# An attention and channel-mix kernel on one core: the first weights asked for in ScalarE's queue, key buffers without gaps, first zero fills on VectorE

## The chip, the cores and the metric

The kernel runs on one core of a Trainium2 chip. The metric is device time in microseconds (us) of one execution, lower is better; the time of the kernel before is the median of three runs. Engines: PE is TensorE (PEld its weight loads), DVE is VectorE, ACT is ScalarE, POOL is GpSimd, SP is SyncE, which here only issues transfers. ACT can issue transfers too, in a queue of its own.

## The reference

Four batches, eight heads, 768 positions, head size 64. Attention with a local window of 96 positions and 8 global positions and a linear position bias, and on its output, with the heads side by side (512 wide), a channel mix:

```
scores = scale * q @ k.T + bias;  scores = where(keep, scores, -1e9)
a = exp(scores - max);  a = a / (sum(a) + 1e-09);  x = a @ v
xk = mu_k * x + (1 - mu_k) * x_prev;  xr = mu_r * x + (1 - mu_r) * x_prev
k = maximum(xk @ w_k, 0);  v = k * k @ w_v;  r = sigmoid(xr @ w_r)
out = r * v
```

w_k is 512 x 1024, w_v 1024 x 512, w_r 512 x 512. They come as float64, two 32-bit words for each number.

## The kernel before

The 3072 positions are 24 tiles of 128 rows. For each tile the queries and keys of all heads are loaded in transposed form (64 partitions, 8 heads x 128), scored on PE two heads at a time (L313, L314), biased and reduced on DVE (L322, with a table `pat`, or `pat0` for the first tile of a batch), exponentiated on ACT (L323), scaled on ACT and POOL (L334, L336), transposed on PE and copied by ACT (L348, L350), and multiplied by v (L367). The first eight tiles ("native") score straight from the loaded tiles: queries go to two buffers `qz`, keys to a ring of three `kz`. These buffers have 128 partitions, of which the loads fill 64; the other 64 are zeroed once (L223, L226, on POOL). Two of the three key buffers are cut out of wider tiles (128 of 232 columns per head), so their rows consist of eight pieces of 512 bytes.

Two tiles make a chunk of the channel mix (`ffn`): mixing with the position before on ACT or POOL and DVE (L391, L393, L394), a split into a high part on ACT (`xk_hi`, L395) and a low part on DVE (`xk_lo`, L396), and then three matmuls for each product (L403 to L405): 96 for `kp` (w_k) and, with 512 columns each, 24 for `z` (w_r) and 48 for `vps` (w_v). Steps of `ffn` are woven between the attention steps of later tiles; the first `ffn` begins with tile 3 (`LAG`).

The weights come in ten loads of 1 MB: four of w_k (`w_0` to `w_3`), two of w_r, four of w_v, each turned from float64 words into two float32 halves by `weight_begin` and `weight_end`: ACT takes the absolute value (L172, L175), POOL (for w_k, L173) or DVE (L176) clamps it, DVE shifts and merges (L177, L178, L179), ACT rounds the high part (L181) and DVE subtracts it (L187). W_LOADS says how many loads are asked for at each step of the program (four steps a tile), W_BEGUN how many are begun.

All loads go through SP's queue, in program order per buffer. A transfer is issued only when a transfer that used the same one of eight counters (every eighth of either queue, about) has landed. The order on each engine is set when the kernel is built, by a scheduler that works with times of its own; on the chip every engine goes through its list strictly in order.

Of the kernel before, what the change touches and what calls it, by code (L numbers as in the profile page):

```python
# [9 lines left out]
F32 = mybir.dt.float32  # L10
F32R = mybir.dt.float32r
BF16 = mybir.dt.bfloat16
I32 = mybir.dt.int32
U32 = mybir.dt.uint32
AF = mybir.ActivationFunctionType
# [4 lines left out]
B, H, S, D = 4, 8, 768, 64  # L20
# [8 lines left out]
W = GMAX + BACK + 128  # L29
# [1 line left out]
LATE = 128 - OWN  # L31
NEG = -1.0e9

W_LOADS = (2, 2, 2, 2, 3, 3, 4, 4, 4, 5, 5, 6, 6, 7, 7, 8, 8, 9, 9, 10)
W_BEGUN = (1, 1, 2, 2, 3, 3, 4, 4, 4, 5, 5, 6, 6, 6, 7, 7, 8, 8, 9, 9, 10)
GAP = {"kk_hi": 16, "xk_lo": 96, "xr_lo": 16}
FAR = 1.0e12
# [4 lines left out]
def tile_biased_attention_channel_mix(ctx: ExitStack, tc: tile.TileContext, qT, kT, v, n_sizes, mu_kr, w_k, w_v, w_r, q_rows, k_rows, v_rows, slopes, out):  # L42
    nc = tc.nc
    vec, act, pool, pe = nc.vector, nc.scalar, nc.gpsimd, nc.tensor

    const = ctx.enter_context(tc.tile_pool(name="const", bufs=1))
# [27 lines left out]
    kw_pool = fast.enter_context(tc.tile_pool(name="kw", bufs=2))  # L74
# [6 lines left out]
    f_pool = fast.enter_context(tc.tile_pool(name="fp", bufs=1))  # L81
# [7 lines left out]
    zeros = const.tile([128, 512], BF16, name="zeros")  # L89
# [5 lines left out]

    pat = const.tile([128, H, W], BF16, name="pat")
    pat0 = const.tile([128, H, 128], BF16, name="pat0")
    f_pool.tile([128, 96], F32, name="ahead", tag="ahead")  # L100
    btmp = f_pool.tile([128, 2048 + GAP["kk_hi"]], F32, name="btmp", tag="kk_hi")
    cut = iter((0, 352, 704, 928, 1056, 1184, 1184 + W))
    edge = [next(cut)]
# [1 line left out]
    def piece():  # L105
        edge.append(next(cut))
        return btmp[:, edge[-2] : edge[-1]]

    ints, flts, local, glo, dist0, dist = (piece() for _ in range(6))
    ints = ints.bitcast(I32)  # L110
    j = flts[:, 224:352]
# [14 lines left out]
    vec.scalar_tensor_tensor(dist0, glo, nlf, local[:, 96:224], op0=ALU.max, op1=ALU.min)  # L126
    for h in range(H):
        c = -8.0 * 2.0 ** -(h + 1)
        if h < 6:
            vec.tensor_scalar(pat0[:, h, :], dist0, c, None, op0=ALU.mult)  # L130
        else:
            pool.tensor_scalar(pat0[:, h, :], dist0, c, 1.0, op0=ALU.mult, op1=ALU.mult)
# [6 lines left out]
    for h in range(H):  # L139
        c = -8.0 * 2.0 ** -(h + 1)  # L140
# [2 lines left out]
        else:  # L143
            pool.tensor_scalar(pat[:, h, :], dist, c, 1.0, op0=ALU.mult, op1=ALU.mult)
    pool.tensor_scalar(mus1, mus, -1.0, 1.0, op0=ALU.mult, op1=ALU.add)

    w_steps = [(name, src, j) for name, src, pairs in (("k", w_k, 4), ("r", w_r, 2), ("v", w_v, 4)) for j in range(pairs)]
    w_raw, w_live = {}, {}

    def weight_load(i):  # L150


        name, src, j = w_steps[i]
        raw = w_raw[i] = const.tile([128, 1024, 2], I32, tag=f"w{i}", name=f"w64_{i}")
        if name == "k":
            ins = nc.sync.dma_start(raw.rearrange("p n w -> p (n w)"), src[j * 128 : (j + 1) * 128, :])
        else:
            ins = nc.sync.dma_start(raw.rearrange("p (k n) w -> p k (n w)", k=2), src[j * 256 : (j + 1) * 256, :].rearrange("(k p) m -> p k m", p=128))
        tc.keep_in_program_order(ins)

    def weight_begin(i):

# [26 lines left out]
            kn = both if name == "k" else both[:, :, k * 512 : (k + 1) * 512]  # L189
            wts[name, j if name == "k" else 2 * j + k] = kn[:, 0, :], kn[:, 1, :]  # L190

    w_count = [0, 0, 0]

    def weights_load(n):
        while w_count[2] < min(n, len(w_steps)):
            weight_load(w_count[2])
            w_count[2] += 1

    def weights_go(begun, ended):
        weights_load(begun)  # L200
        while w_count[0] < min(begun, len(w_steps)):
            weight_begin(w_count[0])
            w_count[0] += 1
        while w_count[1] < min(ended, w_count[0]):
            weight_end(w_count[1])
            w_count[1] += 1
# [11 lines left out]
    q_zero, k_ring = [], []  # L218
    for i in range(3):
        if i < 2:  # L220
            q_zero.append(q_pool.tile([128, H, 128], F32, name=f"qz_{i}", tag="qh"))
            kz = kw_pool.tile([128, H, W], F32, name=f"kz_{i}", tag="kw")[:, :, 0:128]
            pool.memset(q_zero[i][64:128], 0.0)  # L223
        else:
            kz = q_pool.tile([128, H, 128], F32, name=f"kz_{i}", tag="ql")
        pool.memset(kz[64:128], 0.0)  # L226
        k_ring.append(kz)
    k_first = const.tile([64, H, GMAX], F32, name="k_first")

# [244 lines left out]
    for step in range(NTILES + 1):  # L474
        if step + 1 < NTILES:
            load_tile(step + 1)
        if step == 0:
            load_v(0)
        if step < NATIVE:
            first_keys(step)  # L480
        for hp in range(4):
            if hp == 0 and step > 1:
                for i in range(4):
                    weighted(step - 2, i)
            if hp == 0 and 0 < step < NTILES:
                load_v(step)
            if step:
                transposes(step - 1, hp)
            if step < NTILES:
                scores(step, hp)  # L490
            if hp == 0:
                if step >= LAG and (step - LAG) % 2 == 0:
                    queue.append(ffn((step - LAG) // 2))
                    if len(queue) == 1 and step == LAG:
                        budget[0] = -17.5
            run_ffn(2.5)
            run_ffn(2.5)
            if hp == 1 and step + 1 < NTILES:
                split_tile(step + 1)
            slot = 4 * step + hp  # L500
            weights_load(W_LOADS[min(slot, len(W_LOADS) - 1)])
            n = W_BEGUN[min(slot, len(W_BEGUN) - 1)]
            weights_go(n, n - 1 if slot < len(W_BEGUN) else n)
# [172 lines left out]
```

## Time and profile before

| | us |
|---|---|
| median of 3 runs (511.41 to 511.92) | 511.73 |
| the profiled execution, its own time | 511.73 |
| its span, first to last instruction | 510.0 |
| PE busy in the span | 488.9 |
| DVE busy | 346.6 |
| ACT busy | 338.0 |
| POOL busy | 215.3 |

A timeline row has start, duration, engine, line, operation, what is written and read, and in brackets the idle time of the engine before it and what ended that. A duration includes the end of the pipeline, so that instructions in a row overlap a little; what one costs its engine is the distance between two starts. The granted clock of PE is 1.00 at 2.4 GHz and 0.50 at 1.2 GHz.

### The profile page before, as it was taken

Reading aid. Unit: us, or ns where it says so; the run is one execution under the profiler, and the core shown is the slowest. Engines: PE = TensorE matmul, PEld = TensorE weight load, DVE = VectorE, ACT = ScalarE, POOL = GpSimd, SP = SyncE. Lnnn points to the kernel's source line nnn. Section 1 sums busy time; section 2 is a strip of 40 time slices with the busy share of each in tenths; the row PEclk is TensorE's granted clock in tenths of the full one; section 3 lists DMA queues with packets and bytes.
Section 4 is the critical chain, followed back from the end, with each engine's and each line's share of the span. In section 5 each row is a group of like instructions: output and inputs, shape, how many; then the busy total and the mean of one; then the engine's idle time right before and its main releaser. Section 6 shows DMA issues by size and latency. Waiting matters only on the chain.

```text
span 510.0 us, 10113 instructions
## 1 busy us (share of the span) xinstructions
PE 488.9 (96%) x3562; PEld 431.8 (85%) x3562; DVE 346.6 (68%) x826; ACT 338.0 (66%) x826; POOL 215.3 (42%) x359
## 2 busy tenths in 40 slices
PE   7858998999999999999999999999999999999995
PEld 4647987898898898898898898898898898898984
DVE  6999989755468777757768767757768765535321
ACT  4998999757548759567668577567668578554220
POOL 7341216243348546527538536527538535203000
PEclk9888999999999999999999999999999999999999
DMA  8998511513842433433433333433323221100101
GB/s 225 321 247 248 204 42 39 121 43 78 173 91 78 104 101 81 103 100 78 107 84 79 104 102 78 104 100 79 106 82 80 64 60 39 41 1 2 41 2 46
DMA packets 24041, 49.46 MB, mean 97 GB/s; under 512 B 5008, under 2 KB 9104, under 8 KB 23472
## 3 DMA queue, kind: packets, MB, share of 16 engines
q1 hardware_dynamic: 23840, 48.74, 35.5%
q8 instruction: 30, 0.49, 0.4%
q14 instruction: 27, 0.22, 0.1%
q10 hardware_dynamic: 144, 0.00, 0.0%
HBM read 42.44 MB, written 6.29 MB: 96 GB/s over the span
## 4 chain that ended last, share of the span: by engine, by line
PE 85%; DMA 7%; DVE 3%; ACT 2%; issue 1%; POOL 1%; SPq 1%; POOLq 0%; DVEq 0%
PE kp L403 8%; PE vps L405 8%; PE vps L404 8%; PE vps L403 8%; PE kp L405 8%; PE kp L404 8%; PE av L367 7%; PE t L348 7%; DMA qz<-in_qT_dram 5%; PE z L403 4%; PE z L404 4%; PE z L405 4%; PE s L317 3%; PE s L316 3%; PE s L314 2%; PE s L313 1%
## 5 line engine op out<-in xcount | busy, mean ns | idle before, releaser
L336 POOL TENSOR_SCALAR e<-e,r 128x232 f32<-128x232 f32 (+1 forms) x168 | 83.1, 513 | 162.2 <-DVE r L330 130.2
L403 PE MATMUL kp<-xk_hi,wk 128*128 128x256 f32 x384 | 108.4, 283 | 2.0 <-ACT xk_hi L395 2.0
L404 PE MATMUL kp<-xk_lo,wk 128*128 128x256 f32 x384 | 107.3, 280 | 0.0
L405 PE MATMUL kp<-xk_hi,wk 128*128 128x256 f32 x384 | 107.2, 279 | 0.0
L323 ACT ACTIVATE e<-e,nmax 128x232 f32<-128x232 f32 (+1 forms) x192 | 89.6, 470 | 22.7 <-DVE nmax L322 22.1
L322 DVE CUSTOM_DVE_ANT_0 e<-s,pat 128x232 f32<-128x232 f32 (+1 forms) x192 | 64.6, 374 | 22.8 <-PE s L317 14.3
L405 PE MATMUL vps<-wv,kk_lo 128*128 128x512 f32 x192 | 75.3, 392 | 0.0
L403 PE MATMUL vps<-wv,kk_hi 128*128 128x512 f32 x192 | 75.2, 394 | 0.0
L404 PE MATMUL vps<-wv,kk_hi 128*128 128x512 f32 x192 | 75.2, 392 | 0.0
L403 PEld LDWEIGHTS kp<-xk_hi,wk 128*128 128x128 f32 x384 | 72.0, 188 | 3.0 <-ACT xk_hi L395 2.2
L404 PEld LDWEIGHTS kp<-xk_lo,wk 128*128 128x128 f32 x384 | 72.1, 188 | 0.4
L405 PEld LDWEIGHTS kp<-xk_hi,wk 128*128 128x128 f32 x384 | 72.1, 188 | 0.0
L431 DVE TENSOR_TENSOR kk<-kp,kk 128x512 f32<-128x512 f32 x48 | 33.1, 689 | 46.5 <-ACT kk L430 46.3
L350 ACT COPY et<-t 128x256 f32<-128x256 f32 (+1 forms) x176 | 56.3, 373 | 8.2 <-PE t L348 7.6
L348 PE MATMUL t<-ident,e 128*128 128x128 f32 x352 | 54.5, 276 | 0.9 <-ACT e L334 0.7
L348 PEld LDWEIGHTS t<-ident,e 128*128 128x128 f32 x352 | 40.2, 136 | 9.7 <-ACT e L334 0.9
L367 PE MATMUL av<-et,va 128*64 128x128 f32 x384 | 42.7, 287 | 4.4 <-ACT et L350 4.2
L433 DVE TENSOR_TENSOR kk_lo<-kk,kk_hi 128x512 fp32r<-128x512 f32 x48 | 34.6, 722 | 17.5 <-ACT kk_hi L432 17.1
L430 ACT ACTIVATE kk<-kp 128x512 f32<-128x512 f32 x48 | 28.4, 591 | 24.5 <-PE kp L405 24.3
L432 ACT CAST kk_hi<-kk 128x512 fp32r<-128x512 f32 x48 | 29.8, 623 | 20.9 <-DVE kk L431 20.1
L405 PEld LDWEIGHTS vps<-wv,kk_lo 128*128 128x128 f32 x192 | 36.0, 188 | 7.7
L404 PEld LDWEIGHTS vps<-wv,kk_hi 128*128 128x128 f32 x192 | 36.2, 188 | 6.9
(101 smaller groups left out, 1067.0 us busy)
## 6 DMA issues: line engine op xcount, KB each, us to landing
qraw<-in_qT_dram SPq DMA_DIRECT2D x32, 256.0 KB
kraw<-in_kT_dram SPq DMA_DIRECT2D x32, 256.0 KB
out_dram<-sig SPq DMA_DIRECT2D x24, 256.0 KB
va<-in_v_dram SPq DMA_DIRECT2D x20, 240.0 KB
vb<-in_v_dram SPq DMA_DIRECT2D x20, 208.0 KB
w<-in_w_k_dram SPq DMA_DIRECT2D x4, 1024.0 KB
w<-in_w_v_dram SPq DMA_DIRECT2D x4, 1024.0 KB
qz<-in_qT_dram SPq DMA_DIRECT2D x8, 256.0 KB
```

The lines of the kernel that those rows point to most:

```text
L322: vec.tensor_tensor_reduce(out=e[:, :w], in0=o, in1=p[:, h, :], op0=ALU.add, op1=ALU.min, scale=-0.125, scalar=3.0e38, accum_out=s["nmax"] ...
L323: act.activation(e[:, :w], e[:, :w], AF.Exp, bias=s["nmax"][:, h : h + 1], scale=-1.0, accum_out=s["sum"][:, h : h + 1])
L336: pool.tensor_scalar(e[:, :w], e[:, :w], r[:, u : u + 1], 1.0, op0=ALU.mult, op1=ALU.mult)
L348: pe.transpose(pt[0:p, c : c + 128], e[:, k * 128 : k * 128 + p], ident)
L350: act.copy(et[0:p, k * 256 : k * 256 + 256], pt[0:p, k * 256 : k * 256 + 256])
L367: pe.matmul(o, vt[:, h * 64 : (h + 1) * 64], et[0:p, c + q : c + 128], start=k == 0, stop=k == nb - 1)
L403: pe.matmul(o, sh, mh, start=first, stop=False)
L404: pe.matmul(o, sh, ml, start=False, stop=False)
L405: pe.matmul(o, sl, mh, start=False, stop=last)
L431: vec.tensor_mul(kk, pv, kk)
L432: act.copy(kkh[:, 2 * fp : 2 * fp + 2, :], kk)
L433: vec.tensor_sub(kkl[:, 2 * fp : 2 * fp + 2, :], kk, kkh[:, 2 * fp : 2 * fp + 2, :])
```

## The change

The four loads of w_k are issued by ACT instead of SP, all of them ahead of the program's loop and behind a tiny activation (`warm`) that brings the activation table in. W_LOADS asks for w_r and w_v some steps earlier. The two key buffers that were cut from wider tiles are now one run of 1024 columns in the same tiles. Zero fills of the first query and first key buffer go from POOL to DVE. Of the eight heads of `pat0`, the four odd ones go to ACT (three from DVE, one from POOL). Two tiles that only fill space (`ahead`) are added or widened. Moved text is left out here:

```diff
-W_LOADS = (2, 2, 2, 2, 3, 3, 4, 4, 4, 5, 5, 6, 6, 7, 7, 8, 8, 9, 9, 10)
+W_LOADS = (4, 4, 4, 4, 4, 4, 5, 5, 6, 6, 7, 7, 8, 8, 9, 9, 10)
...
+    warm = const.tile([128, 1], F32, name="warm")
+    act.activation(warm, zeros[:, 0:1], AF.Exp)
...
+        raw = w_raw[i] = w_home[i]
         if name == "k":
-            ins = nc.sync.dma_start(raw.rearrange("p n w -> p (n w)"), src[j * 128 : (j + 1) * 128, :])
+            ins = nc.scalar.dma_start(raw.rearrange("p n w -> p (n w)"), src[j * 128 : (j + 1) * 128, :])
...
+    const.tile([128, 96], F32, name="ahead")
+    w_home = [const.tile([128, 1024, 2], I32, tag=f"w{i}", name=f"w64_{i}") for i in range(len(w_steps))]
+    weights_load(4)
...
-    f_pool.tile([128, 96], F32, name="ahead", tag="ahead")
+    f_pool.tile([128, 128], F32, name="ahead", tag="ahead")
...
-        if h < 6:
+        if h % 2:
+            act.mul(pat0[:, h, :], dist0, c)
+        elif h < 6:
             vec.tensor_scalar(pat0[:, h, :], dist0, c, None, op0=ALU.mult)
...
-            kz = kw_pool.tile([128, H, W], F32, name=f"kz_{i}", tag="kw")[:, :, 0:128]
-            pool.memset(q_zero[i][64:128], 0.0)
+            kz = kw_pool.tile([128, H, W], F32, name=f"kz_{i}", tag="kw").rearrange("p h w -> p (h w)")[:, 0 : H * 128]
+            kz = kz.rearrange("p (h w) -> p h w", h=H)
+            (pool if i else vec).memset(q_zero[i][64:128], 0.0)
...
-        pool.memset(kz[64:128], 0.0)
+        (pool if i else vec).memset(kz[64:128], 0.0)
```

The scheduler moves more than the diff says. On SP, from the first weights on, stood this before (`w_0` to `w_3` are w_k, `w_4` and `w_5` w_r; the first `qz_172` row is the queries of tile 2, `qz_176` those of tile 3):

```order
L156 DMA w_0_201<-in_w_k_dram 128x2048
L156 DMA w_1_203<-in_w_k_dram 128x2048
L258 DMA kz_180<-in_kT_dram 64x1024
L270 DMA va_268<-in_v_dram 8x512
L271 DMA va_268<-in_v_dram 120x512
L272 DMA vb_269<-in_v_dram 104x512
L250 DMA qz_172<-in_qT_dram 64x1024
L156 DMA w_2_289<-in_w_k_dram 128x2048
L156 DMA w_3_341<-in_w_k_dram 128x2048
L272 DMA vb_391<-in_v_dram 104x512
L158 DMA w_4_442<-in_w_r_dram 128x2x1024
L158 DMA w_5_498<-in_w_r_dram 128x2x1024
```

and now (`qz_189` is the queries of tile 2, `qz_193` those of tile 3, `kz_190` and `kz_194` the keys of tiles 3 and 4; `w_6` is the first load of w_v):

```order
L282 DMA vb_282<-in_v_dram 104x512
L112 DMA w_4_141<-in_w_r_dram 128x2x1024
L282 DMA vb_401<-in_v_dram 104x512
L112 DMA w_5_142<-in_w_r_dram 128x2x1024
L112 DMA w_6_143<-in_w_v_dram 128x2x1024
L260 DMA qz_189<-in_qT_dram 64x1024
...
L280 DMA va_400<-in_v_dram 8x512
L281 DMA va_400<-in_v_dram 120x512
L268 DMA kz_190<-in_kT_dram 64x1024
L260 DMA qz_193<-in_qT_dram 64x1024
L268 DMA kz_194<-in_kT_dram 64x1024
L260 DMA qz_189<-in_qT_dram 64x1024
```

The queries of tile 2 stood behind two weight loads and now stand behind both of w_r and the first of w_v as well, with the four of w_k in the other queue.

On ACT, ahead of the rounding of the first mixed activations (`xk_hi`), stood this before (`wa_629` is the load `w_6`):

```order
L350 COPY et_0_536<-t_0_535 128x256
L350 COPY et_0_536<-t_0_535 104x256
L350 COPY et_1_581<-t_1_580 128x256
L350 COPY et_1_581<-t_1_580 104x256
L175 ACTIVATE wa_629<-w_6_608 128x1024
L323 ACTIVATE e_2_593,sum_440<-e_2_593,nmax_441 128x232
L395 CAST xk_hi<-mix_k 128x1024
```

and now (`wa_771` is the load `w_7`, `wv_643` the high part of `w_6`):

```order
L197 CAST wv_643<-wa_637 128x1024
L360 COPY et_0_544<-t_0_543 128x256
L360 COPY et_0_544<-t_0_543 104x256
L360 COPY et_1_590<-t_1_589 128x256
L360 COPY et_1_590<-t_1_589 104x256
L344 ACTIVATE e_4_475<-e_4_475,r_3_501 128x232
L344 ACTIVATE e_5_478<-e_5_478,r_3_501 128x232
L191 ACTIVATE wa_771<-w_7_144 128x1024
L405 CAST xk_hi<-mix_k 128x1024
```

`xk_hi` stood behind the absolute value of `w_6`, and now stands behind the rounding of `w_6` and the absolute value of `w_7`.

On DVE, ahead of the low part `xk_lo`, stood this before (`wa_444` is `w_4`, `wa_500` is `w_5`, `wa_629` is `w_6`):

```order
L179 SCALAR_TENSOR_TENSOR wa_444<-w_4_442,wa_444 128x1024
L322 ISA e_4_623,nmax_441<-s_2_618,pat 128x232
...
L176 TENSOR_SCALAR wa_500<-wa_500 128x1024
L322 ISA e_5_626,nmax_441<-s_2_618,pat 128x232
...
L176 TENSOR_SCALAR wa_629<-wa_629 128x1024
L322 ISA e_6_651,nmax_441<-s_3_646,pat 128x232
...
L322 ISA e_7_654,nmax_441<-s_3_646,pat 128x232
...
L177 TENSOR_SCALAR wa_500<-wa_500 128x1024
L396 TENSOR_TENSOR xk_lo<-mix_k,xk_hi 128x1024
```

and now (`wa_637` is `w_6`, `wr_514` the low part of `w_5`, `wa_771` is `w_7`):

```order
L194 SCALAR_TENSOR_TENSOR wa_637<-w_6_143,wa_637 128x1024
L203 TENSOR_TENSOR wr_514<-wa_508,wr_514 128x1024
...
L195 SCALAR_TENSOR_TENSOR wa_637<-w_6_143,wa_637 128x1024
L404 SCALAR_TENSOR_TENSOR mix_k<-x_397,mus,mix_k 128x256 x3
...
L332 ISA e_5_633,nmax_452<-s_2_625,pat 128x232
...
L203 TENSOR_TENSOR wv_643<-wa_637,wv_643 128x1024
L192 TENSOR_SCALAR wa_771<-wa_771 128x1024
L193 TENSOR_SCALAR wa_771<-wa_771 128x1024
L406 TENSOR_TENSOR xk_lo<-mix_k,xk_hi 128x1024
```

Before, `w_4` was not yet subtracted there and `w_5` and `w_6` had only their clamps (and `w_5` its shift); now `w_4`, `w_5` and `w_6` are finished and `w_7` has its clamp and shift, all ahead of `xk_lo`. At the start, ACT has the step of `w_0` (L188 in the new numbering, L172 before) ahead of its first exponential, where it had it behind all eight and two scalings.

## Rows read from the trace of the kernel before

**Rows 1.** The page's heads: the span; busy time of the engines; by 40 slices, the granted clock of PE.

```profile
span 510.0 us, 10113 instructions
...
PE 488.9 (96%) x3562; PEld 431.8 (85%) x3562; DVE 346.6 (68%) x826; ACT 338.0 (66%) x826; POOL 215.3 (42%) x359
...
PEclk9888999999999999999999999999999999999999
```

**Rows 2.** Busy time by stretches of the span: stretch, its length, busy time (instructions) of PE, PEld, DVE, ACT, POOL, granted clock, share of the DMA engines, GB/s.

```profile
10.00:20.00 10.00, 7.23 (x56) 5.94 (x55) 7.66 (x35) 9.90 (x37) 4.02 (x8) 1.00 1.04 321
30.00:40.00 10.00, 5.18 (x35) 4.47 (x36) 9.69 (x17) 9.83 (x27) 5.09 (x6) 0.72 1.06 187
40.00:50.00 10.00, 7.87 (x60) 6.45 (x59) 9.70 (x27) 7.56 (x20) 0.66 (x2) 0.94 0.86 261
60.00:80.00 20.00, 20.00 (x153) 17.68 (x152) 17.93 (x41) 18.93 (x41) 5.61 (x9) 1.00 0.28 82
80.00:100.00 20.00, 18.66 (x137) 15.59 (x136) 16.44 (x42) 16.95 (x46) 8.95 (x14) 1.00 0.37 83
100.00:130.00 30.00, 30.00 (x208) 26.33 (x208) 17.80 (x41) 20.42 (x45) 9.68 (x18) 1.00 0.21 60
160.00:460.00 300.00, 300.00 (x2254) 269.78 (x2253) 206.74 (x488) 203.68 (x500) 146.08 (x246) 1.00 0.31 83
```

**Rows 3.** PE's waits in the first 60 us: line and operand, what ended the wait, us in total, times, the longest.

```profile
PE s L313 <- DMA qz<-in_qT_dram: 4.7, 2, 2.4
...
PE kp L403 <- ACT xk_hi L395: 2.0, 1, 2.0
```

**Rows 4.** The timeline around the first matmuls of the channel mix (`kp`).

```profile
46.53 1.15 ACT L175 ACTIVATE wa<-w 128x1024 f32<-128x1024 f32 x1 [2.44 <-DVE nmax L322]
...
48.05 1.03 ACT L395 CAST xk_hi<-mix_k 128x1024 fp32r<-128x1024 f32 x1
...
49.14 0.63 PE L403 MATMUL kp<-xk_hi,wk 128*128 128x256 f32 x3 [2.01 <-ACT xk_hi L395]
...
49.56 1.22 DVE L396 TENSOR_TENSOR xk_lo<-mix_k,xk_hi 128x1024 fp32r<-128x1024 f32 x1
...
53.35 0.36 PE L404 MATMUL kp<-xk_lo,wk 128*128 128x256 f32 x1
```

**Rows 5.** DVE's timeline at the start: the zeros for the first dummy matmuls, the sizes, six heads of `pat0`, the first bias-and-minimum of tile 0.

```profile
0.87 0.27 DVE L90 MEMSET zeros<- 128x256 uint32 x1 [0.87 <-PEq L666]
...
4.14 0.56 DVE L57 CAST words<-sizes_w 128x4 f32<-128x4 int32 x1 [2.14 <-DMA sizes_w<-in_n_sizes_dram]
...
7.58 1.31 DVE L130 TENSOR_SCALAR pat<-btmp 128x128 bf16<-128x128 f32 x6
...
9.08 0.28 DVE L322 CUSTOM_DVE_ANT_0 e<-s,pat 128x128 f32<-128x128 f32 x1
```

**Rows 6.** ACT's timeline: the table, four heads of `pat`, and the first steps of `w_0` and of `w_3`.

```profile
1.16 1.28 ACT L142 ACT_TABLE_LOAD   x1 [1.16 <-PEq L666]
7.63 1.25 ACT L142 ACTIVATE pat<-btmp 128x232 bf16<-128x232 f32 x4 [5.18 <-DVE btmp L136]
...
13.29 1.13 ACT L172 ACTIVATE wa<-w 128x1024 f32<-128x1024 f32 x1
...
28.37 1.21 ACT L172 ACTIVATE wa<-w 128x1024 f32<-128x1024 f32 x1
```

**Rows 7.** The timeline where SP issues `w_0` and `w_1`, and where PE gets the queries of tile 2 and of tile 3.

```profile
4.40 0.91 SPq L156 DMA_DIRECT2D w<-in_w_k_dram  x2
...
20.16 0.44 PE L313 MATMUL s<-kz,qz 128*128 128x104 f32 x2 [2.37 <-DMA qz<-in_qT_dram]
...
37.73 0.72 PE L313 MATMUL s<-kz,qz 128*128 128x104 f32 x2 [2.37 <-DMA qz<-in_qT_dram]
```

**Rows 8.** Stretches of 1 us, columns as in rows 2: keys and queries of the first tiles under way, then w_k alone, then PE after its wait for tile 3.

```profile
6.00:7.00 1.00, 0.17 (x1) 0.20 (x2) 0.98 (x7) 0.00 (x0) 0.94 (x3) 1.00 0.96 157
...
10.00:11.00 1.00, 1.00 (x8) 1.00 (x7) 0.31 (x4) 1.00 (x6) 0.00 (x0) 1.00 1.08 451
...
38.00:39.00 1.00, 1.00 (x6) 1.00 (x6) 1.00 (x3) 1.00 (x3) 1.00 (x2) 0.50 0.96 158
...
41.00:42.00 1.00, 1.00 (x10) 1.00 (x9) 1.00 (x2) 1.00 (x3) 0.00 (x0) 0.86 1.01 213
```

**Rows 9.** DVE's timeline, instructions back to back: two heads of a later tile, shift, merges and subtraction of weights, and two that took longer than their like.

```profile
18.60 1.00 DVE L329 TENSOR_SCALAR r<-sum 128x4 f32<-128x4 f32 x1
...
26.16 0.39 DVE L322 CUSTOM_DVE_ANT_0 e<-s,pat 128x232 f32<-128x232 f32 x1
26.48 0.40 DVE L322 CUSTOM_DVE_ANT_0 e<-s,pat 128x232 f32<-128x232 f32 x1
...
29.88 2.05 DVE L178 SCALAR_TENSOR_TENSOR wa<-w,wa 128x1024 int32<-128x1024 int32 x1
...
32.49 0.68 DVE L177 TENSOR_SCALAR wa<-wa 128x1024 int32<-128x1024 int32 x1
33.09 0.15 DVE L329 TENSOR_SCALAR r<-sum 128x4 f32<-128x4 f32 x1
33.17 1.21 DVE L179 SCALAR_TENSOR_TENSOR wa<-w,wa 128x1024 int32<-128x1024 int32 x1
34.30 1.21 DVE L178 SCALAR_TENSOR_TENSOR wa<-w,wa 128x1024 int32<-128x1024 int32 x1
```

More of the change, by code (lines that the diff above doesn't have):

```diff
@@ L93, in tile_biased_attention_channel_mix, with weight_load, weights_load @@
         pe.matmul(idle, zeros[:, 0:128], zeros, start=True, stop=True)
+    warm = const.tile([128, 1], F32, name="warm")
+    act.activation(warm, zeros[:, 0:1], AF.Exp)
+    w_steps = [(name, src, j) for name, src, pairs in (("k", w_k, 4), ("r", w_r, 2), ("v", w_v, 4)) for j in range(pairs)]
+    w_raw, w_live = {}, {}
+    def weight_load(i):
+        name, src, j = w_steps[i]
+        raw = w_raw[i] = w_home[i]
+        if name == "k":
+            ins = nc.scalar.dma_start(raw.rearrange("p n w -> p (n w)"), src[j * 128 : (j + 1) * 128, :])
+        else:
+            ins = nc.sync.dma_start(raw.rearrange("p (k n) w -> p k (n w)", k=2), src[j * 256 : (j + 1) * 256, :].rearrange("(k p) m -> p k m", p=128))
+        tc.keep_in_program_order(ins)
+    w_count = [0, 0, 0]
+    def weights_load(n):
+        while w_count[2] < min(n, len(w_steps)):
+            weight_load(w_count[2])
+            w_count[2] += 1
+    const.tile([128, 96], F32, name="ahead")
+    w_home = [const.tile([128, 1024, 2], I32, tag=f"w{i}", name=f"w64_{i}") for i in range(len(w_steps))]
+    weights_load(4)
     pat = const.tile([128, H, W], BF16, name="pat")
     pat0 = const.tile([128, H, 128], BF16, name="pat0")
-    f_pool.tile([128, 96], F32, name="ahead", tag="ahead")
+    f_pool.tile([128, 128], F32, name="ahead", tag="ahead")
     btmp = f_pool.tile([128, 2048 + GAP["kk_hi"]], F32, name="btmp", tag="kk_hi")
@@ L145, in tile_biased_attention_channel_mix @@
     pool.tensor_scalar(mus1, mus, -1.0, 1.0, op0=ALU.mult, op1=ALU.add)
[L147 to L155, printed above, removed]
-            ins = nc.sync.dma_start(raw.rearrange("p n w -> p (n w)"), src[j * 128 : (j + 1) * 128, :])
-        else:
-            ins = nc.sync.dma_start(raw.rearrange("p (k n) w -> p k (n w)", k=2), src[j * 256 : (j + 1) * 256, :].rearrange("(k p) m -> p k m", p=128))
-        tc.keep_in_program_order(ins)
     def weight_begin(i):
@@ L190, in weight_end @@
             wts[name, j if name == "k" else 2 * j + k] = kn[:, 0, :], kn[:, 1, :]
[L192 to L197, printed above, removed]
     def weights_go(begun, ended):
```

## The prediction

> **What bounds the kernel now.** I read the page's heads first: PE is busy for 488.9 of 510.0 us [rows 1], so the time is PE's work plus the stretches in which PE has none. The table by stretches says where those are [rows 2]: from 160 to 460 us PE is busy throughout, and nearly so from 60 on, while up to 50 us it is not. There the view of waits names the queries of tile 2 and 3 (4.7 us in two waits) and `xk_hi` (2.0 us) [rows 3]. The timeline gives the point that matters: with the first `kp` at 49.14 us PE starts to work without a break, since from there attention and channel mix feed it together [rows 4]. What happens before that point only counts through its date. That date is set by DVE and ACT: DVE is busy for 9.7 of 10 us from 30 to 40 and from 40 to 50 [rows 2], with attention and the preparation of weights, and ACT stands for 2.44 us, until 46.53, for the load `w_6` [rows 4]. The DMA engines are at a share of about 1 all that time (1.04 at 10 to 20, 1.06 at 30 to 40) [rows 2].
>
> So I ask one thing of every edit: does it bring the first `kp` with its `xk_lo` earlier, and what does PE do after it?
>
> **The mark before.** The first three `kp` take 0.63 us from 49.14 [rows 4]. In the new order PE has done four more score matmuls of tile 4 by then (half as wide as `kp`, so 4 / 3 / 2 of 0.63, 0.42 us), otherwise the same work. So a first low-part matmul (`kp<-xk_lo`) at 49.14 + 0.63 + 0.42 = 50.2 us would leave the time as it is. Before, that matmul came only at 53.35, but PE had other work until then and was not idle; now it follows the first three directly.
>
> **DVE's work ahead of that mark.** It decides the case. Distances between starts give the costs: a head of 128 x 232 0.32 (26.16 to 26.48), a shift or clamp 0.60 (32.49 to 33.09), a merge 1.13 (33.17 to 34.30), a small one on the sums 0.08 (33.09 to 33.17) [rows 9]. A subtraction and `xk_lo` work on the same 128 x 1024 and I take 1.13 too; a head of 128 x 128 is 0.28 long [rows 5] and overlaps like the large ones (0.39 for 0.32), so 0.21; a mix of 256 columns I put at 0.40, a quarter of 1.13 and a fixed 0.1. Between the first head of tile 0 and `xk_lo` stand, before: 8 small and 24 large heads (9.4), 12 small ones (1.1), 9 shifts or clamps (5.4), 10 merges and 4 subtractions (15.8), 4 mixes (1.6) and two tests (0.4): 33.7 us. From 9.08 [rows 5] to 49.56 [rows 4] are 40.5 us, so DVE lost 6.8 us there to waits and to slow instructions, such as 2.05 for a merge and 1.00 for a small one [rows 9]. In the new order stand there: 8 small and 22 large heads (8.7), 12 small ones (1.1), 12 shifts or clamps (7.2), 14 merges and 7 subtractions (23.7), 4 mixes (1.6): 42.3 us, 8.6 more, since `w_4`, `w_5` and `w_6` are finished ahead of `xk_lo`.
>
> **Edit by edit.** *Zero fills on DVE.* Two fills of 1024 columns, at four times the 0.27 us of 256 columns about 1.07 each, 2.1 us; they lie in DVE's wait of 2.14 us for the sizes and the gap ahead of it [rows 5]: 0, and 2.1 if the sizes came at once. POOL's fills end earlier, and nobody waits for those that are left. *Odd heads on ACT.* DVE does three heads fewer, at 1.31 / 6 each 0.66 us, with two small tests now ahead of its first head: that starts at about 8.6 instead of 9.08 [rows 5]. ACT does four more, between 0.17 and 0.31 us each (the four of `pat` take 1.25 [rows 6]), ahead of `pat`: it comes free at about 9.9 instead of 8.9. *Keys in one piece.* Six loads of 256 KB; with the pieces of 512 bytes under way the rate was 157 GB/s [rows 8], at 190 (30 to 40 us had 187 [rows 2]) each would save 0.3 us. Only the first could matter, and its gain is covered (next step): 0, bounds 0 and 0.3 us earlier. *`warm` and `ahead`.* The table was loaded at 1.16 anyway [rows 6]; 0.
>
> *w_k in ACT's queue.* ACT issues `w_0` when the table is in (2.44), one per 0.45 us [rows 6, 7]; the fourth waits for the sizes at 4.14 [rows 5]. Alone, w_k moved at 451 GB/s [rows 8], 2.3 us per load, and I take 190 for the rest. To the end of `w_3` 4 MB of weights and 1.25 MB of others must pass: 9.3 + 6.6 us after 2.5, so about 19 with its landing; `w_0`, sharing with the first keys, at about 9, `w_1` at 12.5. ACT then takes up `w_0` at 9.9 instead of 13.29 and `w_3` at 20 instead of 28.37 [rows 6]. In the row, one queue already fills the engines (share 1.04), so a second one can only reorder. The Trainium skill, "DMA: Bandwidth & Descriptors", section "Issuing engines are not separate DMA queues", says the same of the two queues; if they did add up, `w_3` would be there near 14, and the sum below would shrink by 0.9.
>
> The queries of tile 2 now lie behind 3 MB more (7 us) and reach PE at about 29 (19 + 7, and 3 for their own way) instead of 20.16 [rows 7]. That costs nothing as DVE's list stands: it reaches the first head of tile 2 only after 25 us of work and most of its waits, at about 37. Behind this, though, hang the keys of tile 4 (they overwrite keys that tile 2 reads) and in SP's list `w_7`, which I expect to land near 50; ACT needs it ahead of `xk_hi` at about 52, so it is nearly late.
>
> **Waits.** ACT has the heads of both patterns and the step of `w_0` ahead of its first exponential, POOL one step after that, and DVE stands from its sixth small head (10.0) to 11.9: 1.9 us. Behind its second merge of `w_1` it stands 0.9 us for the rounding of `w_0`, which ACT has behind the step of `w_2`. For slow instructions like the two of rows 9 I add 1.2. Together 4.0 us; bounds are 0 and the 6.8 of before, and I take the middle since the waits for queries and for `w_6` are gone and that at the start is new.
>
> **The sum.** First head 8.6 + work 42.3 + waits 4.0 + `xk_lo` itself 1.1 = 56.0, against 50.2: +5.8 us. Given back later: DVE and ACT have less to do for weights after that point. Of PE's gaps from 60 to 130 I count the idle 1.3 of 80 to 100 (20.00 - 18.66) [rows 2]. +5.8 - 1.3 = +4.5. The profiled execution took 511.7 us, which is the median of the runs as well: **516.2 us**. PE's clock is priced as a bound only: after its wait for tile 3 PE worked at 0.50, 1.2 GHz [rows 8], from 37.73 [rows 7] to somewhere past 41 [rows 8], 3.5 us that gave half the work; if the first `kp` fell into that state it would cost 1.8 more. PE is idle a good part of the time ahead of it in both cases, and stood at 0.94 on the mean of 40 to 50 [rows 2].
>
> **Rivals.** *A, faster: the weights that are ready early feed PE later.* PEld is a measure of PE's real work: 269.78 / 300 = 0.90 in the steady part, but 0.88 at 60 to 80, 0.78 at 80 to 100 and 0.88 at 100 to 130 [rows 2]; against 0.90 that is 0.3 + 2.4 + 0.7 = 3.4 us that DVE and ACT, full of weights, did not feed. If all came back and DVE had no wait, the sum is +1.8 - 3.4 = -1.6: 510.1. It decides when the waits are under 0.6 us, or when more comes back than PEld shows. Against it: table loads for the sigmoid lie in 80 to 100 and stay. *B, nothing: DVE runs through.* With no waits and the small return, +1.8 - 1.3: 512.2; the second queue then only pays for its own work. The wait that was removed (`w_6`, queries) speaks for it. *C, worse: the first keys come behind all of w_k.* No row shows two queues at work together. If all 4 MB went first, the first keys, there shortly before the head at 9.08 [rows 5], land 9.3 us later, the first exponential comes at about 16.6 instead of 11.0: 516.2 + 5.6 = 522. The Trainium skill, same page, section "Queues, rings and completion order", says that each engine goes round its queues packet by packet; by that the keys would be late by one load at most (2.3 us), ahead of the first exponential still, and the sum would stay at 516.2. No run here shows it yet.
>
> **How the numbers follow.** Chances: forecast 0.60, A 0.20, B 0.12, C 0.08. The forecast's own range is 513 (waits of 1) to 520 (waits of 6.8 and a little of the clock). Down to 510.0 A is included, above 520 C is left out: 510.0 to 520.0. Runs here tell apart about 0.2%, 1 us: faster than 510.7 0.20, within 0.12, slower 0.68.
>
> **What would show it.** In the profile after: ACT's step of `w_0` near 10 and ahead of the first exponential; the first heads of tile 2 on DVE near 37 and not waiting for their queries; `w_4` to `w_6` finished before `xk_lo`; `xk_lo` starting near 55 with PE waiting for it or for `xk_hi`; little idle time of PE from 60 to 130. Wrong I am if `xk_lo` starts before 51, or if PE then loses more than before (a late `w_8`, keys of later tiles).

## The result, and the profile after

The changed kernel takes **519.29 us** (median of 4 runs, 519.21 to 520.3) against 511.57 (511.41 to 511.92): a ratio of 1.0149, 95% interval 1.0131 to 1.0166. It is slower by 7.7 us; 516.2 was forecast, with 510 to 520 as range.

The page's heads of the changed kernel (columns as in [rows 1]):

```profile
span 517.5 us, 10117 instructions
...
PE 487.2 (94%) x3562; PEld 432.3 (84%) x3562; DVE 349.0 (67%) x825; ACT 339.9 (66%) x831; POOL 220.8 (43%) x356
```

PE's work is the same, spread over 7.5 us more. The table by stretches says where (columns as in [rows 2]):

```profile
30.00:40.00 10.00, 1.44 (x7) 1.47 (x8) 10.00 (x21) 8.15 (x20) 3.40 (x3) 0.61 0.87 208
50.00:60.00 10.00, 6.93 (x48) 5.80 (x48) 8.18 (x21) 8.40 (x23) 4.28 (x6) 0.83 0.73 250
60.00:80.00 20.00, 19.38 (x170) 18.59 (x169) 19.47 (x41) 20.00 (x55) 5.74 (x4) 1.00 0.35 109
80.00:100.00 20.00, 20.00 (x133) 16.73 (x133) 15.39 (x39) 18.55 (x38) 7.64 (x16) 1.00 0.30 77
100.00:130.00 30.00, 30.00 (x249) 27.25 (x249) 14.57 (x46) 18.95 (x53) 8.66 (x18) 1.00 0.20 57
```

From 30 to 40 us PE has 1.44 us of work where it had 5.18 [rows 2]; DVE is busy there without a gap. PE's waits in the first 60 us (columns as in [rows 3]):

```profile
PE s L323 <- DMA qz<-in_qT_dram: 8.8, 1, 8.8
PE s L324 <- DMA kz<-in_kT_dram: 6.7, 1, 6.7
```

The first keys are a wait that before did not have, and the queries of tile 2 cost PE 8.8 us in one piece. The timelines: the start on ACT (its three issues of w_k, its step of `w_0`, its first exponential), PE and DVE; where SP issues `w_6` and the queries of tile 2; PE's first scores of tile 2 and DVE's first head of it; where SP issues `w_7` and `w_8`; then the first `kp`:

```profile
1.23 1.36 ACTq L110 DMA_DIRECT2D w<-in_w_k_dram  x3
...
8.92 1.10 ACT L188 ACTIVATE wa<-w 128x1024 f32<-128x1024 f32 x1
13.59 0.40 ACT L333 ACTIVATE e<-e,nmax 128x128 f32<-128x128 f32 x1 [3.57 <-DVE nmax L332]
...
12.02 3.57 PE L324 MATMUL s<-kz,qz 128*128 128x128 f32 x16 [6.68 <-DMA kz<-in_kT_dram]
...
13.25 0.29 DVE L332 CUSTOM_DVE_ANT_0 e<-s,pat 128x128 f32<-128x128 f32 x1 [5.18 <-PE s L324]
...
22.02 0.47 SPq L112 DMA_DIRECT2D w<-in_w_v_dram  x1
22.77 0.48 SPq L260 DMA_DIRECT2D qz<-in_qT_dram  x1
...
38.56 0.72 PE L323 MATMUL s<-kz,qz 128*128 128x104 f32 x2 [8.81 <-DMA qz<-in_qT_dram]
...
42.05 0.39 DVE L332 CUSTOM_DVE_ANT_0 e<-s,pat 128x232 f32<-128x232 f32 x1
...
51.10 0.91 SPq L112 DMA_DIRECT2D w<-in_w_v_dram  x2
...
59.32 1.14 ACT L191 ACTIVATE wa<-w 128x1024 f32<-128x1024 f32 x1 [1.58 <-DMA w<-in_w_v_dram]
60.37 1.04 ACT L405 CAST xk_hi<-mix_k 128x1024 fp32r<-128x1024 f32 x1
...
61.84 1.22 DVE L406 TENSOR_TENSOR xk_lo<-mix_k,xk_hi 128x1024 fp32r<-128x1024 f32 x1
...
61.89 0.60 PE L413 MATMUL kp<-xk_hi,wk 128*128 128x256 f32 x3
...
63.11 0.39 PE L414 MATMUL kp<-xk_lo,wk 128*128 128x256 f32 x1 [0.62 <-DVE xk_lo L406]
```

DVE's first head stands at 13.25 instead of 9.08 [rows 5], `xk_lo` at 61.84 instead of 49.56 [rows 4]: 12.28 us later. Ahead of `xk_hi` ACT has the step of `w_7`, and waits 1.58 us for that load. The same stretch, first head to `xk_lo`, as DVE's busy time, in the kernel before:

```profile
9.08:49.56 40.48, 36.36 (x106) 0.87 1.00 289
```

and in the changed one (stretch, length, busy, granted clock, share of the DMA engines, GB/s):

```profile
13.25:61.84 48.59, 45.32 (x110) 0.77 0.75 225
```

So the 12.28 us are 4.17 of a later first head, 8.96 more of DVE's work, and 0.85 less of standing (4.12 to 3.27). On PE the first `kp<-xk_lo` is 9.8 us later (63.11 against 53.35 [rows 4]), and at the end 7.5 us of span are left.

### The profile page after: what moved, and what is told of

It is laid out like the page before. It is cut to its first block, busy times and chain, and to the rows that moved or that the text cites. A ratio compares the mean times of both kernels' runs of the same rounds, so it can differ in the third digit from the quotient of the medians.

```text
span 517.5 us, 10117 instructions
## 1 busy us (share of the span) xinstructions
PE 487.2 (94%) x3562; PEld 432.3 (84%) x3562; DVE 349.0 (67%) x825; ACT 339.9 (66%) x831; POOL 220.8 (43%) x356
## 5 line engine op out<-in xcount | busy, mean ns | idle before, releaser
L346 POOL TENSOR_SCALAR e<-e,r 128x232 f32<-128x232 f32 (+1 forms) x168 | 89.2, 548 | 172.5 <-DVE r L340 114.6
L358 PE MATMUL t<-ident,e 128*128 128x128 f32 x352 | 56.2, 279 | 6.8 <-ACT e L344 4.6
L388 ACT COPY x<-av 128x512 f32<-128x512 f32 x24 | 14.1, 588 | 42.3 <-PE av L377 42.3
```

Source lines behind the costliest of these rows:

```text
L346: pool.tensor_scalar(e[:, :w], e[:, :w], r[:, u : u + 1], 1.0, op0=ALU.mult, op1=ALU.mult)
L358: pe.transpose(pt[0:p, c : c + 128], e[:, k * 128 : k * 128 + p], ident)
```

## The experiments

Ratios are to the kernel before on the same chip, with their intervals; "beside before" is the ratio less one, times 511.6 us. By that the change itself stands at +7.6. The last two columns are from each timeline of PE: the first scores of tile 0 and the first `kp<-xk_lo`. Each timeline is that of one profiled execution; with w_k later it took 516.69 us and with the queries ahead of `w_4` 529.55, both above the median.

| kernel | ratio (interval) | beside before | first scores | first `kp<-xk_lo` |
|---|---|---|---|---|
| before | | | 6.83 | 53.35 |
| changed | 1.0149 (1.0131 to 1.0166) | +7.6 | 12.02 | 63.11 |
| before, keys in one piece | 0.9982 (0.9966 to 0.9998) | -0.9 | 6.58 | 52.57 |
| before, odd heads | 1.0000 (0.9991 to 1.0009) | 0.0 | 6.80 | 55.97 |
| before, fills | 1.0082 (1.0068 to 1.0095) | +4.2 | 6.76 | 56.26 |
| before, fills and odd heads | 1.0138 (1.0102 to 1.0174) | +7.1 | 6.72 | 60.44 |
| the same, queries ahead of `w_2` | 1.0071 (1.0048 to 1.0094) | +3.6 | 6.75 | 60.05 |
| changed, old table | 1.0088 (1.0058 to 1.0119) | +4.5 | 12.82 | 56.33 |
| changed, w_k later | 1.0052 (1.0035 to 1.0069) | +2.7 | 6.61 | 60.13 |
| changed, w_k later and old table | 1.0096 (1.0073 to 1.0119) | +4.9 | 6.62 | 59.58 |
| changed, first keys first | 1.0101 (1.0086 to 1.0117) | +5.2 | 6.87 | 57.02 |
| changed, no fills, no odd heads | 1.0259 (1.0238 to 1.0281) | +13.3 | 12.51 | 65.25 |
| changed, queries ahead of `w_4` | 1.0278 (1.0248 to 1.0308) | +14.2 | 12.67 | 73.57 |
| changed, `xk_hi` ahead of `w_7` | 1.0167 (1.0147 to 1.0186) | +8.5 | 12.02 | 64.19 |

**Two theories of the changed kernel.** S: the time is lost at the start, since the first keys share the DMA engines with w_k. L: it is lost because weights asked for early are finished ahead of `xk_lo`. Each got a run that undoes its part. *The old table:*

```
-W_LOADS = (4, 4, 4, 4, 4, 4, 5, 5, 6, 6, 7, 7, 8, 8, 9, 9, 10)
+W_LOADS = (4, 4, 4, 4, 4, 4, 4, 4, 4, 5, 5, 6, 6, 7, 7, 8, 8, 9, 9, 10)
```

> The changed kernel (519.3 us) with one part undone: the table of slots asks for w_r and w_v as late as before; w_k stays at once in ScalarE's queue. In this order DVE has 35.9 us of work between its first head and xk_lo by the prediction's prices (42.3 in the changed kernel, 33.7 before), and ACT has xk_hi ahead of its step of w_6, so no load of w_v stands before it. Theory L (the time is lost because DVE and ACT finish w_4 to w_6, and ACT waits for w_7, ahead of xk_lo): xk_lo ends near 55 instead of 63.1, and since less is then given back after that point, the time is 512 to 515 us, say 513.5. Theory S (the time is lost at the start, since the first keys come 5 us later than before behind w_k): DVE's first head stays at 13.2 us and the time stays within 1.5 us of 519.

516.5 us: 3.1 below the change by the ratios. On this list L accounts for that much, short of the 4 to 7 that it promised; `xk_lo` started at 53.94, as it said (55 at its end), but PE's row came at 56.33.

*w_k later,* asked for behind ACT's heads of the first pattern instead of ahead of both patterns:

```
-    weights_load(4)
...
             pool.tensor_scalar(pat0[:, h, :], dist0, c, 1.0, op0=ALU.mult, op1=ALU.mult)
+    weights_load(4)
```

> The changed kernel (519.3 us) with one part moved: the four w_k loads are asked for in ScalarE's queue behind its heads of the first bias pattern, so at about 7.5 us instead of 1.2; the early table for w_r and w_v stays. By the order DVE has 36.6 us of work ahead of xk_lo. Theory S (first keys late behind w_k): the first keys are there by 7, DVE's first head at about 9 instead of 13.2, and the time falls by 4 us or more, to 513 to 515.5. Theory L (weights asked for early are what costs): the first head comes earlier but w_5 and w_6 still lie ahead of tile 2's or tile 3's keys, the list is only 5.7 us shorter by one half of w_5 and w_6 moving out, and the time is 515 to 518. Should both hold, 512 to 514.

514.45 us: 4.9 below the change, as S says. Its timelines of PE, DVE, ACT and PE again:

```profile
6.61 1.13 PE L324 MATMUL s<-kz,qz 128*128 128x128 f32 x8 [1.42 <-DVE btmp L168]
...
7.82 0.28 DVE L332 CUSTOM_DVE_ANT_0 e<-s,pat 128x128 f32<-128x128 f32 x1
...
12.77 1.25 ACT L172 ACTIVATE pat<-btmp 128x232 bf16<-128x232 f32 x4 [4.89 <-DMA va<-in_v_dram]
13.93 0.38 ACT L333 ACTIVATE e<-e,nmax 128x128 f32<-128x128 f32 x1
...
60.13 0.39 PE L414 MATMUL kp<-xk_lo,wk 128*128 128x256 f32 x1
```

PE no longer waits for the keys, and DVE's first head is 5.4 us earlier; the mark on PE gains only 3.0. But this is no clean test of the start. ACT has three issues of w_k between its two patterns and stood 4.89 us there, by the profile until a load of v had landed; its first exponential came at 13.93, no earlier than the 13.59 of the changed kernel. So the 4.9 us of gain are not the earlier first head alone: what else the later w_k moved is in them. *The first keys ahead of w_k in the same queue* is the same test by other means:

```
-                nc.sync.dma_start(kr[o : o + 64], kT[n])
+                (nc.scalar if n == 0 else nc.sync).dma_start(kr[o : o + 64], kT[n])
```

(with the four w_k loads written behind it).

> The changed kernel (519.3 us) with one thing moved: tile 0's keys are asked for in ScalarE's queue too, ahead of w_k, so they needn't share with it. Theory S (of the loss at the first channel mix, 4 us are the first keys that land behind w_0 and beside w_1): first keys at about 6, DVE's first head at 7.5 to 8.5 instead of 13.2, DVE with 37.5 us of work and 4 to 8 of waits starts xk_lo at 50 to 54 instead of 61.8, and the time is 512 to 515. If the start doesn't matter because DVE later waits for tile 2's queries behind the weights: xk_lo starts past 57 and the time is 516 to 519.

516.07, 2.4 below the change by the ratios, with first scores at 6.87, as S says. ACT's timeline:

```profile
9.09 0.39 ACT L332 ACTIVATE e<-e,nmax 128x128 f32<-128x128 f32 x1
```

Here the start is earlier on ACT too. The time lies at the edge of the second expectation, `xk_lo` (54.37) between the two. Undoing the start helped in both runs, by 2.4 to 4.9 us, and this one is the better test of S; but both also gave DVE a shorter list (36.6 and 37.5 us by the prediction's prices) and w_k later, so the share of the start alone isn't separated.

*Both undone:*

> The changed kernel (519.3 us) with two things moved: w_k asked for behind ACT's heads of the first pattern (alone 514.5) and w_r and w_v as late as before (alone 516.5). If the two losses are separate and add: 510.8 to 512.5 us. If they are one loss seen twice (by the order DVE has 36.6 us ahead of xk_lo here as with w_k later alone, and w_4 still lies ahead of tile 2's queries): 513.5 to 515.

516.31, outside both expectations: the losses don't add. It is even 2.2 behind w_k later alone, though DVE's list has the same sum; what the old table costs there no row names.

**The small parts, each alone, on the kernel before.** The one-piece keys (`rearrange("p h w -> p (h w)")[:, 0 : H * 128]`):

> The kernel before (511.6 us) with one part of the change: the key buffers of tiles 0 and 1 in one piece per partition, the same order on every engine. Both theories: the first keys land 0 to 0.5 us earlier than at 6.7 us, the time is within 0.5 us of before. If the pieces of 512 bytes had cost more than that, the time would fall by 1 us or more.

510.84, 0.9 us faster: more than the 0 to 0.3 that I gave them, with an interval that just leaves out no change. It is the one kernel here that beats both. The fills and the heads:

```
-            pool.memset(q_zero[i][64:128], 0.0)
+            (pool if i else vec).memset(q_zero[i][64:128], 0.0)
-        pool.memset(kz[64:128], 0.0)
+        (pool if i else vec).memset(kz[64:128], 0.0)
...
-        if h < 6:
+        if h % 2:
+            act.mul(pat0[:, h, :], dist0, c)
+        elif h < 6:
```

> The kernel before (511.6 us) with two parts of the change: first zero fills on DVE and odd heads of the first pattern on ACT. The order that results has 35.9 us of DVE work ahead of xk_lo instead of 33.7, since w_4 is finished there, and ACT rounds w_4 ahead of xk_hi. By the prediction's sum the first head is at 8.6 to 9.0 and xk_lo ends near 53, 2 us later than before, the time 511.5 to 513.5. If the fills delay the sizes (DVE takes them up later than 4.1 us), the first head comes at 9.5 to 10.5 and the time is 513 to 515.

518.6: a miss by 5 us. The first head did come earlier, at 7.63, so no work of the two parts stands in the way. Apart:

> The kernel before (511.6 us) with one part of the change alone: the first zero fills on DVE. With the odd heads it gave 518.6. In the order that results SP asks for w_2 and w_3 ahead of tile 2's queries, and DVE has 36.6 us ahead of xk_lo (33.7 before), w_4 being finished there. Theory O (what costs is the order that follows from the part, not the part's own work): tile 2's first scores come at 26 to 27 us on PE as with the odd heads, instead of 20.2, xk_lo starts near 55, and the time is 515.5 to 518.5. Theory H (the odd heads load ACT at the start and cost the time): 511 to 512.5.

> The kernel before (511.6 us) with one part of the change alone: odd heads of the first bias pattern on ACT. In the order that results tile 2's queries stay ahead of w_2 and w_3 in SP's list; DVE has 36.0 us ahead of xk_lo. Theory O: first head about 8.0, tile 2's first scores near 20, xk_lo starts at 50 to 52, the time is 511.5 to 513.5. Theory H (the heads on ACT cost the time): 516 to 518.5.

515.13 and 511.25. The heads on ACT cost nothing, although `xk_lo` started at 54.53 with them, not at the 50 to 52 expected. The fills cost 4.2, and not by their own time: DVE's wait for the sizes only shrinks, and its first head is at 8.07. What changed is the list that the scheduler made from it. SP's and PE's timelines with the fills alone:

```profile
9.53 0.83 SPq L156 DMA_DIRECT2D w<-in_w_k_dram  x2
...
15.27 0.48 SPq L250 DMA_DIRECT2D qz<-in_qT_dram  x1
...
27.96 0.72 PE L313 MATMUL s<-kz,qz 128*128 128x104 f32 x2 [1.82 <-DMA qz<-in_qT_dram]
```

`w_2` and `w_3` now lie ahead of the queries of tile 2, which reach PE at 27.96 instead of 20.16 [rows 7]. To see whether that is the cost, fills and heads were kept and every later weight was held behind those queries:

```
-            weight_load(w_count[2])
+            if w_count[2] >= 2 and 2 in q_load:
+                with tc.issue_after(q_load[2].ins):
+                    weight_load(w_count[2])
+            else:
+                weight_load(w_count[2])
```

> The kernel before with zero fills on DVE and odd heads on ACT (518.6 us without more), and one thing moved in SP's list: tile 2's queries ahead of w_2 and w_3. DVE's list ahead of xk_lo becomes longer, 38.4 us instead of 35.9. Theory Q (the 7 us of the two small parts are the queries that lie behind w_2 and w_3): tile 2's first scores at 18 to 20.5 us instead of 26.6, and 511 to 513.5. Theory L (DVE's list decides): xk_lo starts at 54 to 57 and the time is 517 to 520.

```profile
10.58 0.48 SPq L257 DMA_DIRECT2D qz<-in_qT_dram  x1
...
21.79 0.72 PE L320 MATMUL s<-kz,qz 128*128 128x104 f32 x2 [0.26 <-DMA qz<-in_qT_dram]
```

515.06, between the two expectations: 3.5 of the 7.1 us come back although DVE's list grew by 2.5. By this run the queries' place is half of the loss; the other half was not separated. And without fills and heads the changed kernel is not better:

> The changed kernel (519.3 us) without two of its parts: zero fills on GpSimd and all heads of the first pattern where they were; w_k at once in ScalarE's queue, the early table and the one-piece keys stay. DVE has 40.6 us ahead of xk_lo in this order. If w_k at once and the early table cost the time: first head at 13 to 14, xk_lo starts at 57.5 to 60, 516 to 518.5 us. If fills and odd heads were the cause in the changed kernel too, as they are on the kernel before: 511 to 513.

523.79, worse than both expectations, and 5.7 worse than the change. The two parts that together cost 7.1 on one list are worth 5.7 on another. That excludes a fixed price for the pair.

**Two steps of the prediction, one instruction each.** The first: that the late queries of tile 2 cost nothing. The same hold as above, on the changed kernel with `>= 4`:

> The changed kernel (519.3 us) with one thing moved in SP's list: tile 2's queries are asked for ahead of w_4 to w_6 instead of behind them. DVE has the same 42.3 us of work ahead of xk_lo, in nearly the same order. Theory P (the prediction's step: the late queries cost nothing, because DVE's list is full until then): tile 2's first scores come on PE at 22 to 27 us instead of 38.6, DVE's first head of tile 2 still near 40, xk_lo starts at 59.5 to 62, and the time is 518 to 520. Theory Q (attention runs behind tile 2's queries, and that is what costs): xk_lo starts before 58 and the time is 513 to 516.

525.5, 6.6 worse than the change and outside both expectations. Its timelines and waits (PE; SP; ACT's and SP's waits; DVE):

```profile
33.46 0.47 PE L328 MATMUL s<-kz,qz 128*128 128x104 f32 x2 [0.92 <-POOL kz L226]
...
57.66 0.91 SPq L112 DMA_DIRECT2D w<-in_w_v_dram  x2
...
70.65 1.23 DVE L411 TENSOR_TENSOR xk_lo<-mix_k,xk_hi 128x1024 fp32r<-128x1024 f32 x1 [0.96 <-ACT xk_hi L410]
```

```profile
ACT wa L196 <- DMA w<-in_w_v_dram: 4.2, 1, 4.2
...
SPq L273 <- PE s L328: 27.4, 3, 19.1
```

The queries came 5 us earlier to PE (at 33.46, not at the 22 to 27 expected) and `xk_lo` 8.8 us later, so the run doesn't settle the step. What speaks for the step is the changed kernel's own trace: DVE has no gap from 30 to 40, and no wait ahead of its first head of tile 2 at 42.05. In this run SP stood 19.1 us at keys that overwrite what PE still reads, and `w_7` behind it was asked for at 57.66 instead of 51.10. ACT waited 4.2 us for it, ahead of `xk_hi`. Neither theory had that.

The second: that the date of `xk_lo` sets the end. Only ACT's step of `w_7` was moved, behind `xk_hi`:

```
+            with (tc.issue_after(first_hi[0]) if i == 7 else ExitStack()):
+                act.activation(a.bitcast(F32), top.bitcast(F32), AF.Abs, scale=2.0**16)
```

> The changed kernel (519.3 us) with one instruction moved: ACT takes its step of w_7 behind xk_hi instead of ahead of it; all else on ACT, PE and SP stands as it was, and DVE loses two steps of w_7 ahead of xk_lo. ACT can then start xk_hi when it has scaled the heads of tile 2 at 57.7 us, and xk_lo starts at 58.5 to 59.2 instead of 61.84. Theory M (the date of xk_lo, ACT's wait for w_7 in it, is what PE's end follows): 516.3 to 517.3 us. Rival R (PE had scores, transposes and weighted sums of tiles 2 to 4 to do from 56.2 to 61.9 without a break, so only its 0.6 us of waiting for xk_lo comes back): 518.3 to 519.5 us.

```profile
60.53 1.23 DVE L409 TENSOR_TENSOR xk_lo<-mix_k,xk_hi 128x1024 fp32r<-128x1024 f32 x1 [1.27 <-ACT xk_hi L407]
...
62.94 0.60 PE L416 MATMUL kp<-xk_hi,wk 128*128 128x256 f32 x3
```

520.02: `xk_lo` 1.3 us earlier, the first `kp` 1.05 later, the time no better. M, with at most 517.3, falls, since no run of it was under 519.46; R's 518.3 to 519.5 was nearer and missed too. The 1.05 is not the edit's. Up to it the lists of PE, ACT and SP are those of the changed kernel, but PE was already behind, with the weighted sums that follow its wait of 2.61 us at 58.03 instead of 56.21, and its granted clock stayed low for longer (columns as in [rows 2]):

```profile
56.00:58.00 2.00, 1.57 (x8) 1.14 (x6) 2.00 (x10) 1.26 (x3) 1.08 (x3) 0.50 1.02 403
58.00:60.00 2.00, 1.97 (x13) 1.64 (x13) 1.26 (x3) 2.00 (x6) 0.00 (x0) 0.50 0.71 293
60.00:62.00 2.00, 2.00 (x13) 1.74 (x12) 1.47 (x2) 2.00 (x5) 0.26 (x1) 0.58 0.06 18
```

The changed kernel had 0.53, 0.62 and 1.00 there. In both, PE reaches `kp` only behind weighted sums, scores and transposes of tiles 2 to 4, as R says; how late that list would be at the same clock, the two traces don't show. The mark is a row of PE, the later of two lists. In the table the times go roughly with it (about 53: 511 to 512; 56 to 60: 511 to 519; 63 to 65: 519 to 524; 73.57: 525.5), not exactly: with odd heads alone the mark came 2.6 us later than before, at no cost.

## Why the prediction was right in its direction, and where its terms were off

| term | predicted | measured |
|---|---|---|
| DVE's first head | 8.6 | 13.25 |
| DVE's work from there to `xk_lo`, against before | +8.6 | +8.96 (45.32 - 36.36) |
| `xk_lo` starts | 54.9 | 61.84 |
| its end against the mark of 50.2 | +5.8 | +12.9 |
| given back after that | -1.3 | -5.4 |
| profiled execution | +4.5 | +7.5 |

- *The finished weights ahead of `xk_lo`.* Right, to 0.4 us, and the signs that it named are there: `w_0` taken up at 8.92 ahead of the first exponential, DVE reaching tile 2 without waiting (at 42.05, not 37; the queries were at PE at 38.56, not 29). The run with the old table brought 3.1 us of time back.
- *The first keys.* This step failed. I took them to be there before the first head, and put the two queues' turns at one load, 2.3 us; PE got them 5.2 us later than before (12.02 against 6.83). I had ACT ask for `w_0` behind the activation table, at 2.44; it did so at 1.23, and w_k then ran alone until 5.2 us and took turns with the queries and keys after that (last section). Rival C had the mechanism and too large a size (9.3). Moving w_k back or the keys forward brought 6.61 and 6.87.
- *Waits.* 4.0 us, slow instructions included, were 6.3: 48.59 from first head to `xk_lo`, less the 42.3 of work. The wait behind ACT's step of `w_7` (2.3 in the view of DVE's waits) is the largest; the prediction called that load "nearly late" and gave it nothing. Yet the run that took it out of the way gained nothing in time, though its PE, on a lower clock, was late by itself.
- *The mark and the return.* Mis-sized as well, in the other direction. On PE's own rows only 2.3 us come back, from 9.8 at the first `kp<-xk_lo` to 7.5 at the end; the other 3.1 of the 5.4 are the mark of 50.2, which the kernel before never met on PE (53.35 [rows 4]). As to what came back: from 60 to 130 us PEld does 62.57 us where it did 59.60 (sums of three rows above and of [rows 2]), 2.97 more, 3.3 us of time at 0.90, which looks like rival A's sum (3.4). But the run with the old table, and the kernel before with fills and odd heads, do as much (in this order):

```profile
60.00:130.00 70.00, 69.97 (x547) 62.66 (x546) 53.68 (x128) 59.04 (x144) 26.01 (x42) 1.00 0.31 94
60.00:130.00 70.00, 70.00 (x539) 62.48 (x534) 52.29 (x124) 54.92 (x133) 27.51 (x42) 1.00 0.32 94
```

The first asks for w_r and w_v as late as before, the second for every weight in SP's queue. So it isn't shown that early weights feed PE later; A stays open.

- *What lies between.* Two mistakes of some 7 us (the date of `xk_lo`) and 4 (mark and return) cancelled in part. The interval held, but the forecast was better than its working.
- *Edits at nothing.* For fills and heads "0" holds for their own time only. Each also makes the scheduler write another list, and for the fills on the kernel before that alone was 4.2 us. The prediction read the list of the whole change, so it had this effect in its sum without knowing which edit it came from.

What stays open: how the 7.6 us divide among the parts. Each run that undoes one writes new lists on all engines, and they neither add (w_k later and old table) nor keep their sign (fills and heads).

## What to carry to other kernels

A large load in a second queue is not free because the engines are full anyway: ask what small load, needed first, it now shares them with, and write that one ahead of it. An engine that also computes can stand behind the loads that it issues (4.89 us with w_k later). Where a scheduler writes the lists, price an edit by its list and not by its instructions, and try each part alone, since a part that costs nothing to run can cost 4 us by what it moves. Before betting on one date, look for the list on the bound engine that leads to it: here `xk_lo` could come earlier without PE being there to use it.

## What the runs showed of the hardware

The table by stretches of the changed kernel once more, finer:

```profile
5.00:10.00 5.00, 0.34 (x2) 0.00 (x0) 2.96 (x21) 3.04 (x9) 2.44 (x6) 0.83 1.03 299
10.00:15.00 5.00, 2.98 (x13) 2.96 (x14) 1.02 (x8) 1.43 (x8) 1.24 (x2) 0.50 1.03 283
...
56.00:58.00 2.00, 1.79 (x12) 1.46 (x13) 2.00 (x9) 1.74 (x6) 0.52 (x2) 0.53 0.97 352
58.00:60.00 2.00, 2.00 (x14) 1.79 (x13) 0.17 (x1) 0.68 (x1) 0.24 (x1) 0.62 0.60 246
```

Two queues at work together gave no more than one: 299 and 283 GB/s at a share of 1.03, where w_k alone had 451 [rows 8]. The Trainium skill, "DMA: Bandwidth & Descriptors", section "Issuing engines are not separate DMA queues", says so, and the trace agrees.

How they share was new to me. The DMA queues of the changed kernel, from 2 to 5.2 us and from 5.2 to 12 us (packets, MB, share of 16 engines; q10 is ACT's queue, q1 SP's):

```profile
q10 hardware_dynamic: 188, 0.88, 84.1%
q1 hardware_dynamic: 126, 0.00, 1.8%
...
q10 hardware_dynamic: 193, 1.32, 69.9%
q1 hardware_dynamic: 192, 0.66, 33.0%
```

Up to 5.2 us w_k moved alone, although SP asked for the first queries at 1.20 and ACT for `w_0` at 1.23. In the kernel before SP's queue had moved 0.56 MB by then. Why the queries began so late, no run shows. From 5.2 us on the queues took turns, 193 packets to 192, and ACT's moved twice the bytes, since a row of w_k is 8192 bytes and one of keys or queries 4096. The same page of the Trainium skill, section "Queues, rings and completion order", has the engines go round the queues packet by packet; from 5.2 us on the trace agrees. My conclusion from that rule, one load of delay at most, was wrong: w_k had a start of 0.88 MB, most of a load, and after it each row of the first queries and keys (two loads of 256 KB) went beside a row of w_k of twice its size.

The clock made PE's late stretch longer. In the changed kernel PE waited 2.61 us, until 54.53, for ACT, and worked at 0.53 from 56 to 58 and 0.62 from 58 to 60, near the lower of its two levels, 1.2 of 2.4 GHz. By an estimate from these two rows, its busy 1.79 and 2.00 us there would have been 1.6 us less at full clock. That alone would not have brought the mark forward: PE waited 0.62 us for `xk_lo` as it was. The kernel before stood at 1.00 from 50 to 60:

```profile
50.00:60.00 10.00, 10.00 (x88) 9.44 (x87) 10.00 (x19) 9.72 (x28) 1.87 (x2) 1.00 0.62 206
```
